# Full-attention layers: VectorE's queued pieces placed by an estimate of when TensorE finishes, and its own tiles' values planned a microsecond later

## The chip, the cores and the metric

One core of a Trainium2 chip runs the whole kernel: four layers of attention over 2048 tokens. The metric is the device time of one execution in microseconds (us). TensorE appears as PE (matmul) and PEld (weight load), VectorE as DVE, ScalarE as ACT, GpSimd as POOL, SyncE as SP.

## What is computed

The input x is 2048 x 512. Layers 0 and 2 attend in a sliding window of 256 tokens (A), layers 1 and 3 to all tokens (B). Each has 32 heads of 16 and adds its output to x:

```python
x = A_x
x = x + _A_ref(_layernorm(x, axis=-1), A_wqkv, A_wo)
x = x + _B_ref(_layernorm(x, axis=-1), B_wqkv, B_wo)
x = x + _A_ref(_layernorm(x, axis=-1), A_wqkv, A_wo)
x = x + _B_ref(_layernorm(x, axis=-1), B_wqkv, B_wo)
```

In `_B_ref`, per head:

```python
scores = jnp.einsum("bhqd,bhkd->bhqk", q, k) * scale
p = _softmax(scores, axis=-1)
o = jnp.einsum("bhqk,bhkd->bhqd", p, v)
```

## The kernel before

**Tiles of a full layer.** The work of a full layer is cut into 32 quads: 4 heads by one block of 512 queries, written (layer, block of queries, quad of heads) or as `1_3_4` in the names of tiles. Layer 1 goes block by block, layer 3 takes two quads of heads at a time through all four blocks. A quad goes through the 16 tiles of 128 keys (j). For each j there are two pairs of heads; each pair is one scores tile `s` of 128 x 1024 (8 matmuls, L760), which ACT turns into `e` by an exp (L768). Behind it follow the values of that j: 8 matmuls with the tile of V into the two accumulators `acc` (`values_of`, L839). The `s` tiles have two buffers in PSUM. When a quad's last values are in, `epilogue` reads the accumulators into `sa` on DVE (`join`, L438 and L439), transposes and scales.

**VectorE's own tiles.** One tile of keys, j = 7, can be taken off ACT: `unit` writes its scores to the single PSUM bank `halves` (called b in the profile, L778), DVE reads them (`d`, L784) and computes the exp by a polynomial, in two halves of six instructions (dm, d, dp, dp, dp, d, L792 to L804). Together with the reading an own tile is 13 DVE instructions, and a quad has at most two. `units` starts the next own tile if the planner still finds time before the quad's end. If two are in, their values are issued by `unit_values` as soon as the planner's clock has passed `u["at"]`, which is set from DVE's planned clock (L806: `vt_[0] + 0.4`), or, at the latest, right ahead of the quad's last values (`force`). If the second one isn't there three steps before the end, ACT makes it (`e <- s, lead`), and both values follow last.

**Side work.** Projections of this and the next layer, output projections (`wo`, `wo_part`) and the sums of squares for the bounds of the softmax run between the tiles. In a full layer each writes the same bank `halves`, which DVE must read (`j`, `vt`, `x`, `m`, `km`) before the next group may start. `Side` deals out one or two matmul groups of this work per step.

**What sets the order.** In the full layers PE's and DVE's instructions stand in the order in which the program's generators issue them. A planner keeps two clocks: `clock[0]`, PE's, is advanced by estimates (`spent`), and `vt_[0]`, DVE's, by `vec(us)`. DVE work that nothing waits for at once (halves of own tiles, scaling, norms, checks of the weights) is queued as pieces in five queues `VQ` by rank; `drain()` issues pieces while `vt_[0] <= clock[0] + AHEAD`, and a reading of a PSUM tile is issued directly, with a `vec` ahead of it:

```python
    def vec(us):

        vt_[0] = max(vt_[0], clock[0]) + us
...
        while vt_[0] <= clock[0] + AHEAD:
            order = VQ[:2] + VQ[3:4] if PH["mid"] else VQ if not UX or UX[0]["i"] <= PH["i"] else VQ[:3] + VQ[4:] + VQ[3:4]
            q = next((q for q in order if q and (q[0][2] is None or q[0][2]())), None)
            if q is None:
                return
            give(q)
```

All engines issue in order, so a reading whose operand PE has not finished holds up every piece behind it, and values whose operand DVE has not finished hold up every matmul behind them.

Of the kernel before, what the change touches and what calls it, by code (L numbers as in the profile page):

```python
# [39 lines left out]
WS = 16.0  # L40
W_MIN, W_MAX = 2.0 ** -7, 4.0
DJ = 7
AHEAD = 0.7
# [152 lines left out]
def fast_path(ctx, tc, flag, a_x, a_wqkv, a_wo, b_wqkv, b_wo, out):  # L196
# [34 lines left out]

        return "wait", clock[0] + us

    def vec(us):

        vt_[0] = max(vt_[0], clock[0]) + us

    def soon(chain, us, f, ok=None):

# [11 lines left out]
    def drain(upto=None):  # L251

        if upto is not None:
            if PH["mid"] and upto > 2:
                give(VQ[3])
            for q in VQ[:upto]:
                while q:
                    while q[0][2] and not q[0][2]():
                        PH["side"].one(True)
                    give(q)  # L260
            return
        while vt_[0] <= clock[0] + AHEAD:
            order = VQ[:2] + VQ[3:4] if PH["mid"] else VQ if not UX or UX[0]["i"] <= PH["i"] else VQ[:3] + VQ[4:] + VQ[3:4]
            q = next((q for q in order if q and (q[0][2] is None or q[0][2]())), None)
            if q is None:
                return
            give(q)

    def turns(chain, *ops):

# [161 lines left out]
                PH["busy"] = False  # L432
    TERMS = ((0, 0), (0, 1), (1, 0))

    def join(dst, ps, scale=1 / WS):

        vec(1.4)
        nc.vector.tensor_scalar(dst, ps[0], scale, None, op0=ALU.mult)  # L438
        nc.vector.scalar_tensor_tensor(dst, ps[1], scale, dst, op0=ALU.mult, op1=ALU.add)  # L439

# [119 lines left out]
    def squares(n, sqs):  # L560

        drain(1)
        vec(1.4)
        ph = bank()
        for t, sq in sqs.items():
            if PH["full"]:
                for r in range(2):
                    nc.tensor.matmul(ph[32 * t:32 * t + 32, r], hsum[R * r:R * r + R], sq[R * r:R * r + R],
                                     start=True, stop=True, skip_group_check=True)
            else:  # L570
                nc.tensor.matmul(ph[32 * t:32 * t + 32, :], hsum, sq, start=True, stop=True, skip_group_check=True)
        return ph
# [98 lines left out]
    def wo(l, c, tail):  # L671

        w = weights(l % 2, 3, f"o{l}_{c}")
        xs = load_x(l, c)
        yield wait(8)
        for i in range(4):
            ps = bank()
            yield from mms(ps, [(O[l, c, t][:, a, i * P:(i + 1) * P], w[:, t, b, :]) for t in range(NHT) for a, b in TERMS])
            k = 4 * c + i
            with tc.high_priority(HEAD_START):  # L680
                for p in ((ps[:, 0], ps[:, 1]) if PH["full"] else (ps,)):
                    nc.vector.scalar_tensor_tensor(xs[i], p, 1 / WS, xs[i], op0=ALU.mult, op1=ALU.add)
            nc.sync.dma_start(xd[k], xs[i])
            vec(1.4)
            soon(2, 0.9, lambda i=i: stats(l + 1, c, i, xs[i]))
            if i == 3 and not PH["full"]:
                yield from norm(l + 1, c, xs, tail)
            yield -MM if PH["full"] else -12 * MM
        OFREE.update((l, c, t) for t in range(NHT))
        if PH["full"]:  # L690
            yield from norm(l + 1, c, xs, tail)

    def wo_part(c, t):

        w = wp.tile([P, NC, 2, D], F16, name=f"wo_{c}_{t}", tag="w", bufs=WB)[:, 0]
        nc.sync.dma_start(w, wd[1, 3][:, t])
        xs = load_x(3, c)
        yield wait(4)
        o = O.pop((3, c, t))
        for i in range(4):  # L700
            ps = bank()
            yield from mms(ps, [(o[:, a, i * P:(i + 1) * P], w[:, b, :]) for a, b in TERMS])
            vec(1.4)
            k = 4 * c + i
            with tc.high_priority(HEAD_START):
                for p in ((ps[:, 0], ps[:, 1]) if PH["full"] else (ps,)):
                    nc.vector.scalar_tensor_tensor(xs[i], p, 1 / WS, xs[i], op0=ALU.mult, op1=ALU.add)  # L707
            nc.sync.dma_start(out[0, k * P:(k + 1) * P, :] if t == NHT - 1 else xd[k], xs[i])
            if i == 3:
                OFREE.add((3, c, t))  # L710
            yield -MM

    def epilogue(l, c, qd, a):

        n = f"{l}_{c}_{qd}"
        t, u = divmod(qd, 2)
        drain(2)
        ot = vp.tile([P, QC // 32, 32], F32, name=f"ot{n}", tag="oe", bufs=3)  # L720
        with tc.high_priority(HEAD_START if l % 2 else 0):
            if l % 2:
                a = vp.tile([P, QC], F32, name=f"sa{n}", tag="j")
                join(a, acc, 1.0)
                vec(0.7)
            nc.vector.transpose(ot.rearrange("p b r -> p (b r)"), a)  # L726

        def scaled():
            den = ot[:, :, DH]
            nc.vector.tensor_tensor(lmin, lmin, den, ALU.min)  # L730
            nc.vector.tensor_add(lsum, lsum, den)
            r = vp.tile([P, QC // 32], F32, name=f"r{n}", tag="r")
            nc.vector.tensor_scalar_max(r, den, L_MIN)
            nc.vector.reciprocal(r, r)
            if u == 0:
                OT[t] = vp.tile([P, QC // 32, 2, DH], F32, name=f"op{n}", tag="op", bufs=1)
            nc.vector.tensor_tensor(OT[t][:, :, u, :], ot[:, :, :DH], r[:, :, None].broadcast_to([P, QC // 32, DH]), ALU.mult)

        def parts():
            o = vp.tile([P, QC], F32, name=f"o{n}", tag="oe", bufs=3)  # L740
            nc.vector.transpose(o, OT.pop(t).rearrange("p b u d -> p (b u d)"))
            OL.append((l, c, t))
            hl = O[l, c, t] = wp.tile([P, 2, QC], F16, name=f"oh{n}", tag="ohl", bufs=OB)
            nc.vector.tensor_copy(hl[:, 0], o)
            nc.vector.tensor_tensor(hl[:, 1], o, hl[:, 0], ALU.subtract)
            ONR[l, c, t] = clock[0] + 4.5
        soon(1, 1.1, scaled)
        if u:
            soon(1, 1.6, parts, lambda: len(OL) < OB or OL[-OB] in OFREE)
# [21 lines left out]
    def unit(u):  # L771
# [8 lines left out]
        spent(0.27)  # L780
        PH["free"] = clock[0] + 1.5
        t = PH["ep"].tile([P, 2, QC], I32, name=f"d{n}", tag="d", bufs=2)
        vec(1.3)
        nc.vector.tensor_scalar(t, ps, SCALE * LOG2E * 2.0 ** 23, -2.0 ** 30, op0=ALU.mult, op1=ALU.max)  # L784
        u["e"].append(t.bitcast(F32))
        u["left"] += 2
# [55 lines left out]
    def unit_values(l, c, qd, force=False):  # L842
# [3 lines left out]
            return False  # L846
        if force:
            complete(u)
        elif len(u["e"]) < 2 or u["left"] or clock[0] < u["at"]:
            return False  # L850
        UX.popleft()
        values_of(l, qd, DJ, u["e"], False, False)
# [265 lines left out]
    def attention(l, works):  # L1118
# [5 lines left out]
        for t in range(NHT if l == 3 else 1):  # L1124
            for c in range(NQ):
                qds = range(2 * t, 2 * t + 2) if l == 3 else range(NQD)
                if l == 1:

                    sd = sd or Side((NT - 1) * NQD // 2, works[0], works[1], 0.33)
                    while ("Q", 1, c) not in DONE:  # L1130
                        sd.one(True)
                    settle()
                else:
# [44 lines left out]
                    ops = nxt  # L1178
                if l != 1 or c == NQ - 1:
                    sd.finish(l == 3 and (t, c) != (NHT - 1, NQ - 1))  # L1180
                if not win:
                    settle()
        flush(0)
        drain(5)
# [202 lines left out]
```

## Time and profile before

| What | us |
|---|---|
| Median of 3 runs | 2833.18 |
| Lowest and highest | 2832.88, 2838.49 |
| The profiled execution | 2838.99 |
| Its span, first to last instruction | 2837.2 |
| Mean granted TensorE clock over the span | 0.98 |

The span divides into layer 0 and setup (to about 495 us), layer 1 (to 1461), layer 2 (to 1808) and layer 3 with the end (to 2837). The groups of instructions by line give 2304 exps (L768), 22 exps with `lead`, and 106 own tiles (L784). "Idle before" a group is time in which its engine stood still, and the name behind an arrow is the instruction whose semaphore ended it. Only waits on an engine that others wait for in turn cost time.

### The profile page before, as it was taken

How to read it: one execution, taken by the hardware profiler on the slowest of the kernel's cores; microseconds unless marked ns; L12 is line 12 of the kernel's file. 1: busy time of each engine (PE TensorE's matmuls, PEld its weight loads, DVE VectorE, ACT ScalarE, POOL GpSimd, SP SyncE). 2: the span in 40 equal slices, each digit the busy share in tenths (PEclk: the TensorE clock that was granted, in tenths of full speed). 3: DMA queues.
4: the chain of work that ended last, by engine and by line, in shares of the span. 5: the costliest groups of instructions: out<-in, count | busy, mean ns of one | idle time of the engine just before them, and what ended most of it. 6: DMA issues, size and time to landing. Idle time of an engine off the chain costs nothing.

```text
span 2837.2 us, 112864 instructions
## 1 busy us (share of the span) xinstructions
PE 2528.1 (89%) x50177; PEld 1102.0 (39%) x50177; DVE 1991.0 (70%) x3817; ACT 2285.2 (81%) x2581; POOL 474.6 (17%) x1047
## 2 busy tenths in 40 slices
PE   7889999999998999999888899899899899888886
PEld 3333444444333444444333334434344344333332
DVE  5564454586778868878776566567778767777786
ACT  4565654999999998999865665699889889888886
POOL 1445551000000000000024776000000000000000
PEclk9999999999999999999999999999999999999999
DMA  8888856223223224223336654422332323333333
GB/s 274 237 234 238 242 178 203 60 78 108 87 88 96 66 96 109 92 83 103 103 116 207 170 151 140 141 83 87 94 92 88 94 85 101 95 100 105 123 104 122
DMA packets 335043, 359.71 MB, mean 127 GB/s; under 512 B 113617, under 2 KB 250321, under 8 KB 328145
## 3 DMA queue, kind: packets, MB, share of 16 engines
q1 hardware_dynamic: 334544, 352.40, 41.0%
q8 instruction: 394, 6.46, 0.9%
q14 instruction: 105, 0.85, 0.1%
HBM read 239.60 MB, written 96.99 MB: 119 GB/s over the span
## 4 chain that ended last, share of the span: by engine, by line
ACT 36%; PE 33%; DVE 16%; issue 9%; DMA 3%; POOL 2%; SPq 1%; ACTq 0%; DVEq 0%; POOLq 0%
ACT e L768 36%; PE b L425 9%; PE acc L839 9%; PE s L760 4%; PE b L422 3%; PE acc L941 3%; PE bs L425 2%; PE s L764 2%; DVE dp L803 1%; DVE dp L799 1%; DVE d L784 1%; DVE x L707 1%; DVE d L804 1%; DVE dp L800 1%; POOL e L931 1%
## 5 line engine op out<-in xcount | busy, mean ns | idle before, releaser
L768 ACT ACTIVATE e<-s 128x1024 f32<-128x1024 f32 (+2 forms) x2304 | 2138.4, 1044 | 257.8 <-PE s L760 139.5
L839 PE MATMUL acc<-e,vt 64*17 64x512 f32 x15536 | 1069.4, 593 | 0.2 <-issue 0.2
L760 PE MATMUL s<-qt,kt 64*32 64x512 f16 x15536 | 827.6, 382 | 114.7 <-ACT e L768 90.0
L760 PEld LDWEIGHTS <-kt 64*32 64x32 f16 x15536 | 376.8, 90 | 835.7 <-issue 759.4
L839 PEld LDWEIGHTS acc<-e,vt 64*17 64x17 f32 x15536 | 271.2, 93 | 86.7 <-issue 28.4
L934 POOL TENSOR_SCALAR_AFFINE_SELECT e<-e 128x256 f32<-128x256 f32 x512 | 220.8, 437 | 213.0 <-ACT e L768 211.8
L931 POOL TENSOR_SCALAR_AFFINE_SELECT e<-e 128x256 f32<-128x256 f32 x448 | 195.4, 443 | 116.7 <-ACT e L768 115.3
L941 PE MATMUL acc<-e,vt 128*17 128x384 f32 (+2 forms) x2816 | 205.8, 398 | 5.2 <-POOL e L931 4.0
L546 POOL TENSOR_TENSOR sq_h<-sp_h 128x512 bf16<-128x512 f16 x27 | 39.7, 1471 | 924.0 <-DVE sp_h L540 812.8
L546 POOL TENSOR_TENSOR sq<-sp 128x512 bf16<-128x512 f16 x28 | 40.9, 1461 | 868.0 <-DVE sp L540 795.4
L784 DVE TENSOR_SCALAR d<-b 128x1024 int32<-128x1024 f32 x106 | 129.3, 1220 | 79.0 <-PE b L778 78.8
L764 PE MATMUL s<-qt,kt 64*128 64x384 f16 (+2 forms) x1408 | 128.5, 280 | 56.0 <-ACT e L768 35.7
L425 PE MATMUL b<-xc,w 128*128 128x512 f16 x696 | 165.4, 389 | 6.2 <-DMA w<-wd 5.0
L803 DVE SCALAR_TENSOR_TENSOR dp<-dp,dm 128x512 f32<-128x512 f32 x212 | 152.3, 718 | 6.2
L799 DVE SCALAR_TENSOR_TENSOR dp<-dm 128x512 f32<-128x512 f32 x212 | 151.7, 715 | 0.2
L800 DVE SCALAR_TENSOR_TENSOR dp<-dp,dm 128x512 f32<-128x512 f32 x212 | 146.7, 692 | 7.4
L804 DVE SCALAR_TENSOR_TENSOR d<-dp,d 128x512 f32<-128x512 f32 x212 | 146.7, 692 | 7.2
L438 DVE TENSOR_SCALAR sa<-acc 128x512 f32<-128x512 f32 x64 | 44.2, 691 | 144.8 <-PE acc L839 144.3
L839 PE MATMUL acc<-d,vt 64*17 64x512 f32 x848 | 100.0, 606 | 38.3 <-DVE d L804 37.3
L425 PEld LDWEIGHTS <-w 128*128 128x128 f16 x816 | 77.4, 100 | 123.0 <-issue 37.5
L726 DVE STREAM_TRANSPOSE ot<-acc 128x512 f32<-128x512 f32 x64 | 45.6, 713 | 104.8 <-PE acc L941 104.8
L422 PE MATMUL b<-wo,oh 64*32 64x512 f16 x2592 | 111.3, 384 | 7.5 <-DVE x L707 4.6
(151 smaller groups left out, 2575.7 us busy)
## 6 DMA issues: line engine op xcount, KB each, us to landing
kt<-kf SPq DMA_DIRECT2D x128, 512.0 KB
qt<-qs SPq DMA_DIRECT2D x128, 256.0 KB
xd<-x SPq DMA_DIRECT2D x96, 256.0 KB
x<-xd SPq DMA_DIRECT2D x96, 256.0 KB
w<-wd SPq DMA_DIRECT2D x22, 1024.0 KB
kt<-kw SPq DMA_DIRECT2D x64, 256.0 KB
qs<-sp SPq DMA_DIRECT2D x48, 256.0 KB
wo<-wd SPq DMA_DIRECT2D x12, 1024.0 KB
```

The lines of the kernel that those rows point to most:

```text
L422: nc.tensor.matmul(ps[g:g + 32, r], a[k, g:g + 32], b[k], start=(i == 0), stop=(i == len(pairs) - 1), skip_group_check=True)
L425: nc.tensor.matmul(ps, a, b, start=(i == 0), stop=(i == len(pairs) - 1))
L760: nc.tensor.matmul(ps[g:g + 32, h], kt[R * h:R * h + R, pr, kc + g:kc + g + 32], qt[R * h:R * h + R, pr], start=True, stop=True, skip_grou ...
L764: nc.tensor.matmul(ps[:, h, s0:s0 + wd_], kt[R * h:R * h + R, pr, kc:kc + P], qt[R * h:R * h + R, pr, qc:qc + wd_], start=True, stop=True)
L768: nc.scalar.activation(e[:, :, w0:w1], ps[:, :, w0:w1], AF.Exp, scale=SCALE, **bias)
L799: nc.vector.scalar_tensor_tensor(p[0], f, POLY[3], f, op0=ALU.add, op1=ALU.mult)
L800: nc.vector.scalar_tensor_tensor(p[0], p[0], POLY[2], f, op0=ALU.add, op1=ALU.mult)
L803: nc.vector.scalar_tensor_tensor(p[0], p[0], POLY[1], m[0].bitcast(F32), op0=ALU.add, op1=ALU.mult)
L839: nc.tensor.matmul(acc[r][32 * h:32 * h + DH + 1, :], V[l, qd // 4, j // 8][k, j % 8, 4 * (qd % 4) + h, :], es[h // 2][k, h % 2, :], start ...
L931: nc.gpsimd.affine_select(v, v, pattern=[[0, 2], [-1, P]], compare_op=ALU.is_gt, fill=0.0, base=0, channel_multiplier=1)
L934: nc.gpsimd.affine_select(v, v, pattern=[[0, 2], [1, P]], compare_op=ALU.is_ge, fill=0.0, base=0, channel_multiplier=-1)
L941: nc.tensor.matmul(a[32 * h:32 * h + DH + 1, q * P:(q + nb) * P], V[l, (4 * c + j) // 4][:, j % 4, 4 * qd + h, :], es_[h // 2][:, h % 2, s ...
```

## The change

`vec` gets a second argument, the time after `clock[0]` at which the operand is estimated to be finished. In full layers it first issues queued pieces for as long as DVE's planned clock stays 0.4 us short of that time, and then books DVE as busy from that time on; in the windowed layers only the booking is done. The search for the next piece becomes a function, `give_next`, that `drain` uses too. The readings get these estimates: 1.3 us for joins, 2.0 for the join of `sa`, 1.0 for squares and x, 0.8 for own tiles; in `wo` the `vec` now also stands ahead of the reading, not behind it. The values of own tiles are held back until 1.0 us past `u["at"]`. Two calls of `settle` no longer happen while a side group is under way.

```diff
-    def vec(us):
-
-        vt_[0] = max(vt_[0], clock[0]) + us
+    def vec(us, after=0.0):
+
+        if PH["full"]:
+            while after and vt_[0] + 0.4 < clock[0] + after and give_next():
+                pass
+        vt_[0] = max(vt_[0], clock[0] + after) + us
...
-        while vt_[0] <= clock[0] + AHEAD:
-            order = VQ[:2] + VQ[3:4] if PH["mid"] else VQ if not UX or UX[0]["i"] <= PH["i"] else VQ[:3] + VQ[4:] + VQ[3:4]
-            q = next((q for q in order if q and (q[0][2] is None or q[0][2]())), None)
-            if q is None:
-                return
+        while vt_[0] <= clock[0] + AHEAD and give_next():
+            pass
+
+    def give_next():
+
+        order = VQ[:2] + VQ[3:4] if PH["mid"] else VQ if not UX or UX[0]["i"] <= PH["i"] else VQ[:3] + VQ[4:] + VQ[3:4]
+        q = next((q for q in order if q and (q[0][2] is None or q[0][2]())), None)
+        if q is not None:
             give(q)
+        return q is not None
...
-    def join(dst, ps, scale=1 / WS):
-
-        vec(1.4)
+    def join(dst, ps, scale=1 / WS, after=1.3):
+
+        vec(1.4, after)
...
         drain(1)
-        vec(1.4)
+        vec(1.4, 1.0)
         ph = bank()
...
+            vec(1.4, 1.0)
             with tc.high_priority(HEAD_START):
...
             nc.sync.dma_start(xd[k], xs[i])
-            vec(1.4)
...
-            vec(1.4)
             k = 4 * c + i
+            vec(1.4, 1.0)
...
-                join(a, acc, 1.0)
+                join(a, acc, 1.0, 2.0)
...
-        vec(1.3)
+        vec(1.3, 0.8)
...
-        elif len(u["e"]) < 2 or u["left"] or clock[0] < u["at"]:
+        elif len(u["e"]) < 2 or u["left"] or clock[0] < u["at"] + 1.0:
...
-                    while ("Q", 1, c) not in DONE:
+                    while ("Q", 1, c) not in DONE or pend and PH["busy"]:
...
-                if not win:
+                if not win and not PH["busy"]:
                     settle()
```

What it does to the order, at three places. The numbers at the ends of the names are those of the buffers; lines of the change stand 3 to 7 higher. First DVE at the end of quad (3,1,5), in layer 3: `d` are the own tiles 0 and 1 of the quad, `x` and `km` readings of the bank, `sa` the reading of the accumulators. Before:

```order
L707 SCALAR_TENSOR_TENSOR x3_2_46792<-b3_33668,x3_2_46792 128x512 x2
L792 TENSOR_SCALAR dm3_1_5_1_0_48105<-d3_1_5_1_47820 128x512
L793 TENSOR_SCALAR d3_1_5_1_47820<-d3_1_5_1_47820 128x512
L587 TENSOR_REDUCE km3_31320<-b3_33668 32x1
L799 SCALAR_TENSOR_TENSOR dp3_1_5_1_0_48141<-dm3_1_5_1_0_48105 128x512
L800 SCALAR_TENSOR_TENSOR dp3_1_5_1_0_48141<-dp3_1_5_1_0_48141,dm3_1_5_1_0_48105 128x512
L803 SCALAR_TENSOR_TENSOR dp3_1_5_1_0_48141<-dp3_1_5_1_0_48141,dm3_1_5_1_0_48105 128x512
L804 SCALAR_TENSOR_TENSOR d3_1_5_1_47820<-dp3_1_5_1_0_48141,d3_1_5_1_47820 128x512
L792 TENSOR_SCALAR dm3_1_5_1_1_48188<-d3_1_5_1_47820 128x512
```

After the last of these rows come five more of the second half of tile 1, and then `sa`. In the changed program:

```order
L806 SCALAR_TENSOR_TENSOR dp3_1_5_0_1_47801<-dm3_1_5_0_1_47790 128x512
L807 SCALAR_TENSOR_TENSOR dp3_1_5_0_1_47801<-dp3_1_5_0_1_47801,dm3_1_5_0_1_47790 128x512
L714 SCALAR_TENSOR_TENSOR x3_2_46612<-b3_33518,x3_2_46612 128x512 x2
L810 SCALAR_TENSOR_TENSOR dp3_1_5_0_1_47801<-dp3_1_5_0_1_47801,dm3_1_5_0_1_47790 128x512
L811 SCALAR_TENSOR_TENSOR d3_1_5_0_47597<-dp3_1_5_0_1_47801,d3_1_5_0_47597 128x512
L594 TENSOR_REDUCE km3_31170<-b3_33518 32x1
L714 SCALAR_TENSOR_TENSOR x3_3_46614<-b3_33518,x3_3_46614 128x512 x2
L445 TENSOR_SCALAR sa3_1_5_48045<-acc0_81 128x512
```

Tile 1 of this quad is no longer DVE's; ACT has an exp more (`e3_1_5_7_1<-s3_1_5_7_1,lead`), and `x3_3` is read ahead of `sa`, not behind it.

Second, PE at the end of layer 1, behind the last scores of quad (1,3,7): `b` is the bank, `w2_1_2` the weights of a projection for layer 2, `hsum` and `sq` the sums of squares that end it. Before, the 176 matmuls of the projection begin behind the scores:

```order
L760 MATMUL s1_3_7_15_1_28912<-qt1_3_7_27522,kt1_3_7_1_27526 32x512
L422 LDWEIGHTS w2_1_2_27609
L422 MATMUL b1_5731<-xc2_2_27668,w2_1_2_27609 32x512
L422 LDWEIGHTS w2_1_2_27609
L422 MATMUL b1_5731<-xc2_2_27668,w2_1_2_27609 32x512
```

In the changed program:

```order
L767 MATMUL s1_3_7_15_1_28993<-qt1_3_7_27621,kt1_3_7_1_27625 32x512
L575 LDWEIGHTS hsum_86
L575 MATMUL b1_5731<-sq2_1_2_0_27822,hsum_86 32x512
L575 LDWEIGHTS hsum_86
L575 MATMUL b1_5731<-sq2_1_2_0_27822,hsum_86 32x512
```

The projection's matmuls have moved into earlier quads of layer 1, and the squares follow the scores at once.

Third, DVE at the beginning of quad (3,0,2): `o` and `oh` are pieces that finish the heads' output of the quad before, `x3_6` a reading of the bank. Before:

```order
L737 TENSOR_TENSOR op3_3_0_38654<-ot3_3_1_39354,r3_3_1_39564 128x16x16
L707 SCALAR_TENSOR_TENSOR x3_6_37856<-b3_33668,x3_6_37856 128x512 x2
L741 STREAM_TRANSPOSE o3_3_1_39617<-op3_3_0_38654 128x512
L744 CAST oh3_3_1_39619<-o3_3_1_39617 128x512
L745 TENSOR_TENSOR oh3_3_1_39619<-o3_3_1_39617,oh3_3_1_39619 128x512
```

In the changed program:

```order
L744 TENSOR_TENSOR op3_3_0_38542<-ot3_3_1_39189,r3_3_1_39399 128x16x16
L748 STREAM_TRANSPOSE o3_3_1_39411<-op3_3_0_38542 128x512
L751 CAST oh3_3_1_39413<-o3_3_1_39411 128x512
L752 TENSOR_TENSOR oh3_3_1_39413<-o3_3_1_39411,oh3_3_1_39413 128x512
L714 SCALAR_TENSOR_TENSOR x3_6_37706<-b3_33518,x3_6_37706 128x512 x2
```

The piece of three instructions has gone ahead of the reading.

## The prediction

> **What bounds the kernel now.** I read the page's share lines first, then the chain, then stretches of the span by stage, and then who waits for whom inside the full layers, since the edited branches act only there.
>
> ```profile
> PE 2528.1 (89%) x50177; PEld 1102.0 (39%) x50177; DVE 1991.0 (70%) x3817; ACT 2285.2 (81%) x2581; POOL 474.6 (17%) x1047
> ACT 36%; PE 33%; DVE 16%; issue 9%; DMA 3%; POOL 2%; SPq 1%; ACTq 0%; DVEq 0%; POOLq 0%
> ```
>
> No engine holds the chain alone. The stages are more telling. In each row below stand the length of the stretch and then, per engine, its busy time and instruction count, the granted TensorE clock, and the DMA share. The rows are the 32 quads of layer 1, the end of layer 1, and the 32 quads of layer 3.
>
> ```profile
> 495.00:1447.00 952.00, 878.85 (x21969) 390.09 (x21976) 737.89 (x1361) 902.34 (x973) 38.73 (x29) 0.99 0.29 90
> 1447.00:1461.00 14.00, 8.87 (x251) 4.13 (x228) 9.36 (x16) 1.56 (x2) 3.58 (x5) 1.00 0.52 171
> 1808.00:2820.00 1012.00, 892.35 (x21622) 390.07 (x21613) 763.06 (x1298) 904.84 (x971) 39.72 (x27) 0.98 0.32 97
> ```
>
> ACT is busy 902 of 952 us in layer 1 and 905 of 1012 in layer 3, so ACT sets the pace, and its idle time (50 and 107 us) is what can be won. An exp tile costs ACT 902.34 / 973 = 0.93 us. Next, who makes ACT wait, first in layer 1 (495 to 1447 us), then in layer 3 (1808 to 2820 us); and for what PE waits in layer 3. The columns are total us, times, longest us.
>
> ```profile
> ACT e L768 <- PE s L760: 46.5, 37, 10.5
> ...
> ACT e L768 <- PE s L760: 93.0, 52, 6.9
> ...
> PE acc L839 <- DVE d L804: 25.9, 13, 3.2
> ```
>
> ACT waits for scores, and PE, which issues in order, brings them late when it stands before the values of a tile that VectorE still works on (d). One such place, quad (3,1,5), with the clock before, during and behind the wait, on PE, DVE, ACT:
>
> ```profile
> 2424.07 1.99 PE L839 MATMUL acc<-d,vt 64*17 64x512 f32 x12
> 2428.61 0.70 PE L839 MATMUL acc<-d,vt 64*17 64x512 f32 x2 [2.54 <-DVE d L804]
> ...
> 2427.86 0.69 DVE L804 SCALAR_TENSOR_TENSOR d<-dp,d 128x512 f32<-128x512 f32 x1
> 2431.90 0.69 DVE L438 TENSOR_SCALAR sa<-acc 128x512 f32<-128x512 f32 x1 [3.34 <-PE acc L839]
> ...
> 2432.39 3.83 ACT L768 ACTIVATE e<-s 128x1024 f32<-128x1024 f32 x4 [6.91 <-PE s L760]
> ...
> 2417.00:2424.00 7.00, 6.23 (x154) 2.59 (x142) 6.68 (x11) 7.00 (x9) 0.00 (x0) 1.00 0.37 115
> 2424.00:2428.60 4.60, 2.07 (x28) 0.23 (x8) 4.38 (x8) 1.49 (x2) 0.00 (x0) 1.00 0.62 205
> 2428.60:2433.00 4.40, 4.39 (x60) 1.96 (x61) 1.00 (x2) 0.60 (x1) 0.00 (x0) 0.61 0.01 4
> ```
>
> DVE finishes d at 2428.5, 4.5 us after PE began on its values. PE waits 2.54 us, then runs at a granted clock of 0.61 for 4.4 us, and ACT loses 6.91 us. A quad with one own tile ends otherwise: compare its last 12 us with the same stretch of (3,1,5).
>
> ```profile
> 2455.00:2467.00 12.00, 11.21 (x296) 4.98 (x295) 5.04 (x8) 11.72 (x13) 1.15 (x1) 1.00 0.43 123
> 2424.00:2436.00 12.00, 8.74 (x144) 3.11 (x132) 7.78 (x14) 5.09 (x6) 0.00 (x0) 0.86 0.32 102
> ```
>
> With one own tile ACT is idle only 12 - 11.72 = 0.28 us. So the waits sit at the ends of quads in which DVE has two own tiles.
>
> **The change, part by part.** The order of the changed program, counted per quad, says what the planner's numbers do. Own tiles fall from 106 to 93: quads with two of them from 20 to 11 in layer 1 and from 22 to 19 in layer 3.
>
> *ACT's added tiles.* 13 at 0.93 us: **+12.1 us**, 9.3 in layer 1 and 2.8 in layer 3. ACT bounds, so nothing hides them. DVE loses 13 x 13 instructions, off the bound.
>
> *Quads that lose an own tile.* Eleven in layer 1 and five in layer 3. These are ACT's waits at their ends, in order of time, where they pass 1.8 us (six of the eleven; the others hold under 1 us each and count nothing):
>
> ```profile
> 555.84 2.86 ACT L768 ACTIVATE e<-s 128x1024 f32<-128x1024 f32 x3 [1.82 <-PE s L760]
> 938.50 3.78 ACT L768 ACTIVATE e<-s 128x1024 f32<-128x1024 f32 x4 [2.37 <-PE s L760]
> 1086.15 4.69 ACT L768 ACTIVATE e<-s 128x1024 f32<-128x1024 f32 x5 [1.93 <-PE s L760]
> 1119.92 1.02 ACT L768 ACTIVATE e<-s 128x1024 f32<-128x1024 f32 x1 [4.93 <-PE s L760]
> 1240.06 5.61 ACT L768 ACTIVATE e<-s 128x1024 f32<-128x1024 f32 x6 [3.50 <-PE s L760]
> 1364.42 3.77 ACT L768 ACTIVATE e<-s 128x1024 f32<-128x1024 f32 x4 [10.53 <-PE s L760]
> 2053.16 3.77 ACT L768 ACTIVATE e<-s 128x1024 f32<-128x1024 f32 x4 [2.83 <-PE s L760]
> 2177.97 3.77 ACT L768 ACTIVATE e<-s 128x1024 f32<-128x1024 f32 x4 [3.59 <-PE s L760]
> 2495.54 1.02 ACT L768 ACTIVATE e<-s 128x1024 f32<-128x1024 f32 x1 [4.61 <-PE s L760]
> 2562.52 3.77 ACT L768 ACTIVATE e<-s 128x1024 f32<-128x1024 f32 x4 [5.78 <-PE s L760]
> ```
>
> Layer 1: 25.1 us. Layer 3, with the 6.91 above: 23.7 us. What a one-tile quad keeps, 0.28 x 11 = 3.1, goes off: **-45.7 us**. I take nearly all of it because DVE loses 13 instructions in each such quad: the two readings and eleven more that stood between the last scores and d.
>
> *Quads that gain an own tile.* Three: (1,2,5), (3,2,4), (3,3,4). A quad of layer 3 carries 93.0 / 32 = 2.9 us of ACT waits on the mean: **+8.7 us**. Bounds are 0.28 and 6.91 each.
>
> *The end of layer 1.* In the row 1447 to 1461 ACT does two tiles in 14 us while PE works off a leftover projection in two bursts with a DVE reading between them:
>
> ```profile
> 1447.04 2.35 PE L422 MATMUL b<-xc,w 64*32 64x512 f16 x80
> 1451.25 2.78 PE L422 MATMUL b<-xc,w 64*32 64x512 f16 x96 [1.86 <-DVE j L439]
> 1455.58 0.40 PE L568 MATMUL b<-sq,hsum 64*32 64x512 bf16 x6 [1.54 <-DVE j L439]
> 1457.71 0.39 PE L568 MATMUL b<-sq,hsum 64*32 64x512 bf16 x2 [1.74 <-POOL sq L546]
> 1457.72 1.24 PE L839 MATMUL acc<-e,vt 64*17 64x512 f32 x16
> ...
> 1460.61 0.50 PE L764 MATMUL s<-qt,kt 64*128 64x384 f16 x4
> ```
>
> In the changed order the sums of squares follow the last scores directly: these 176 matmuls now stand inside earlier quads. What stays is a few tenths for the squares, the wait for the last exp (about 1 us, one tile), and the values from 1457.72 to 1460.6, 2.9 us. That would take some 4.3 of the 14 us, so at most -9.7. DVE's last own tile had 10 us of cover here that is gone, so PE may wait about 2 us for it, as above. I take **-8 us**, bounds -9.7 and -5. The moved matmuls cost PE 2.35 + 2.78 = 5.1 us in the quads; ten more ACT tiles there give it 9.3 us, so I put them at nothing, and at +5.1 if that cover fails.
>
> *Readings and pieces in quads that keep their tiles.* The edit to `vec` cuts both ways. It hands out pieces while the reading is estimated not to be ready, but it also books VectorE as busy until then, so that the next drains hand out fewer. In the changed order of layer 3, 30 of the 64 x readings stand ahead of pieces that they stood behind, against one that moved the other way; three ends of quads got a piece ahead of `sa`. What DVE waits for over the whole span:
>
> ```profile
> DVE sa L438 <- PE acc L839: 144.3, 54, 8.7
> DVE d L784 <- PE b L778: 78.8, 70, 11.1
> DVE x L707 <- PE b L422: 22.0, 16, 2.7
> ```
>
> A piece before `sa` at the end of a quad fills part of a 2.7 us wait (144.3 / 54); an x read earlier may add a wait of up to a piece, but it also frees the one bank sooner. I take nothing for the sum. Below it: of ACT's 46.5 + 93.0 us, 48.8 are already counted, and half of the other 90.7 would be -45. Above it: see the slower rival. The values a microsecond later and the check on PH["busy"] touch only a few quads; their matmuls are the same, and I put them at nothing between -3 and +3 (the 1 us by three quads).
>
> **Sum**: 12.1 - 45.7 + 8.7 - 8 = -33 us. Against the profiled execution's 2838.99 (its span of 2837.2 and 1.8 around it) that is 2806; that execution lay 5.8 above the median of the runs shown, 2833.18, so the median to expect is **2800**.
>
> **The rivals.**
>
> 1. *The stalls move on* (17%). The quads with fewer own tiles are fine, but ones that keep two get later, since a changed plan shifts DVE's backlog instead of shrinking it. For it: DVE is busy 763 of 1012 us in layer 3 and each own tile still has to pass between readings. Against it: 13 x 13 instructions fewer. If half of the 45.7 comes back elsewhere, the sum is -10: 2823.
>
> 2. *Slower: readings placed earlier make d late* (18%). The x readings that now pass pieces make DVE wait, and 27 quads that keep two own tiles get d later by the piece passed, one to two instructions of the 0.69 us above, say 0.9 us. ACT's loss per us of PE wait is 6.91 / 2.54 = 2.7 at the worst; with 2, 27 x 0.9 x 2 = +49: 2849. It decides once most x readings wait: now 16 waits hold 22.0 us. It would undo the gain from about 33 / 49, two thirds of those quads. This is also the case in which the change doesn't do what its words say, as pieces would not go out ahead of readings.
>
> 3. *More* (15%). The filled waits before `sa`, j and vt bring d forward in the quads that keep two tiles, and half of the 90.7 us goes as well: -78, or 2755. I give it 2770 as its centre, since most such quads keep their order row for row.
>
> 4. PE as the bound instead of ACT would make the 13 tiles free and the 176 matmuls cost 5.1: -33 - 12.1 + 5.1 = -40, 2793, inside my own band. PE's 878.85 busy of 952 speaks for it; that ACT is busy 11.72 of 12 us at an undisturbed end of a quad speaks against it.
>
> 5. *A wait costs only itself* (10%). If PE came back from its waits at full speed, the five quads of layer 3 would yield PE's mean wait, 25.9 / 13 = 2.0 us each, 10 instead of 23.7 us, and the sum would be -19: 2814. Against it: the clock of 0.61 right behind a wait of 2.54 us, and 6.91 us lost by it. The Trainium skill, TensorE: Matmul & The Clock Gate, section "What's actually happening", states the rule on the other side: the clock halves only after an idle window of about 3.4 us, so that waits of 2 us would leave it whole. This trace differs from that, with 0.61 behind 2.54 us.
>
> **How the numbers follow.** The forecast, 2780 to 2818, has 50% (rivals 4 and 5 lie in it, the latter with 10 of the 50), "more" 15%, "moves on" 17% and slower 18%. A difference of 0.2%, 5.7 us, is about what a measurement of this kernel can tell from no change. Faster by that holds the forecast, "more", and half of "moves on": 0.73; the rest of that and the foot of the slower case are the same: 0.10; slower 0.17. The range leaves out a tenth on each side: it goes down into "more", to 2765, and up into the slower case, to 2843.
>
> **What would show it.** Right: ACT's waits on scores fall from 139.5 us in both full layers to about 95, the exp count rises by 13, ACT's busy time in each full layer rises by 9 and 3 us, and the 14 us stretch at the end of layer 1 shrinks to some 6. At the ends of quads (1,3,4), (3,1,5) and (3,3,5) ACT runs through at clock 1.00. Wrong: PE's waits on d in layer 3 stay at 25.9 us or rise, x readings wait far more than 22 us, or the new stretch behind layer 1's last scores holds a long wait for d. More ACT tiles than 13, or a PE wait for the bank that DVE reads later, would break the sum too.

## The result and the profile after

The changed kernel takes 2821.02 us (median of 5 runs, 2819.82 to 2824.31), the kernel before 2833.18 (5 runs, 2829.08 to 2838.49): a ratio of 0.9957, interval 0.9942 to 0.9972. It is 12 us faster; the forecast was 33, and 2800. The profiled execution of the changed kernel took 2821.02 us too, with a span of 2819.3 and a mean clock of 0.983. Lines of the changed kernel stand 7 higher than those of before. Its page, shares and chain:

```profile
PE 2520.6 (89%) x50177; PEld 1098.9 (39%) x50177; DVE 1885.5 (67%) x3648; ACT 2297.9 (82%) x2594; POOL 478.2 (17%) x1047
ACT 41%; PE 31%; DVE 12%; issue 9%; DMA 3%; POOL 2%; SPq 1%; ACTq 0%; DVEq 0%; POOLq 0%
```

ACT has its 13 exps more and 12.7 us more of busy time, DVE 106 us less. Next, by stretch, with the columns as in the prediction: layer 1 up to its last scores, the stretch behind them, and layer 3.

```profile
495.00:1449.40 954.40, 881.88 (x22152) 393.52 (x22160) 670.79 (x1257) 912.34 (x982) 41.96 (x31) 1.00 0.30 93
1449.40:1457.10 7.70, 4.49 (x64) 0.86 (x44) 4.72 (x9) 1.23 (x2) 0.45 (x2) 0.91 0.21 70
1797.00:2801.00 1004.00, 890.91 (x21598) 388.31 (x21597) 735.73 (x1259) 907.34 (x973) 40.02 (x27) 0.99 0.32 98
```

ACT's busy time rose by 10 us in layer 1 and by 2.5 in layer 3 (9 and 3 were forecast), and the stretch behind layer 1's last scores went from 14 to 7.7 us (some 6 were forecast). But layer 3 still leaves ACT idle for 1004.00 - 907.34 = 97 us, after 107. Who waits for whom over the whole span:

```profile
DVE sa L445 <- PE acc L846: 140.9, 51, 8.6
ACT e L775 <- PE s L767: 120.3, 77, 7.4
...
DVE x L714 <- PE b L429: 44.2, 36, 2.9
...
PE acc L846 <- DVE d L811: 40.7, 22, 3.4
```

ACT's waits fell from 139.5 to 120.3 us, not to 95. The readings of x wait twice as long as before (22.0 in 16 waits), and PE waits for d no less than before: 26.5 us in layer 3 after 25.9, and 40.7 over the span after 37.3. The prediction had named both as signs of being wrong.

**Where the time went.** The start of one `sa` reading to the start of the next is a quad's own time, and the quads can be sorted by what happened to their own tiles. The table sums these times over the profiled executions; the first quad of layer 1 has no such time, and that of layer 3 is in the last row. A second execution of the kernel before (e5) and the run that settled the matter (e14, below) stand beside it.

| Quads | before | e5 | after | after - before | forecast | e14 |
|---|---|---|---|---|---|---|
| 16 that lose an own tile | 506.0 | 505.8 | 476.6 | -29.4 | -45.7 + 14.9 = -30.8 | 473.6 |
| 3 that gain one | 92.2 | 91.7 | 92.5 | +0.3 | +8.7 - 2.8 = +5.9 | 90.5 |
| last quad of layer 1 | 39.1 | 39.2 | 33.3 | -5.8 | -8 | 30.9 |
| 24 that keep two | 739.1 | 736.1 | 757.2 | +18.1 | 0 | 731.6 |
| 17 that keep one | 502.2 | 502.0 | 507.6 | +5.4 | 0 | 501.2 |
| end of layer 1 to first `sa` of layer 3 | 378.8 | 375.7 | 371.1 | -7.7 | 0 | 369.5 |

With 1.1 us more in the last quad of layer 3 this gives -18.0, the difference of the two spans (2837.2 and 2819.3). That is more than the 12 us between the medians, because the profiled execution of the kernel before lay 5.8 us above its median. The forecast for the ACT tiles is put where it belongs, 0.93 us for each quad that lost or gained. The sum of the first three rows came nearly as forecast, -34.9 after -32.9. The two rows of quads that keep their tiles cost 23.5 us where the prediction took nothing.

### The profile page after: what moved, and what is told of

It is laid out like the page before. It is cut to its first block, busy times and chain, and to the rows that moved or that the text cites. A ratio compares the mean times of both kernels' runs of the same rounds, so it can differ in the third digit from the quotient of the medians.

```text
span 2819.3 us, 112722 instructions
## 1 busy us (share of the span) xinstructions
PE 2520.6 (89%) x50177; PEld 1098.9 (39%) x50177; DVE 1885.5 (67%) x3648; ACT 2297.9 (82%) x2594; POOL 478.2 (17%) x1047
## 4 chain that ended last, share of the span: by engine, by line
ACT 41%; PE 31%; DVE 12%; issue 9%; DMA 3%; POOL 2%; SPq 1%; ACTq 0%; DVEq 0%; POOLq 0%
ACT e L775 41%; PE b L432 10%; PE acc L846 7%; PE s L767 4%; PE acc L948 3%; PE b L429 3%; PE s L771 2%; PE bs L432 2%; DVE dp L810 1%; POOL e L938 1%; DVE d L811 1%; POOL e L941 1%; DVE dp L807 1%; DVE x L714 1%; DVE dp L806 1%
## 5 line engine op out<-in xcount | busy, mean ns | idle before, releaser
L775 ACT ACTIVATE e<-s 128x1024 f32<-128x1024 f32 (+2 forms) x2304 | 2139.2, 1045 | 233.6 <-PE s L767 120.3
L846 PE MATMUL acc<-e,vt 64*17 64x512 f32 x15640 | 1083.6, 591 | 1.3 <-DVE sa L445 1.3
L791 DVE TENSOR_SCALAR d<-b 128x1024 int32<-128x1024 f32 x93 | 113.4, 1220 | 92.5 <-PE b L785 92.5
L810 DVE SCALAR_TENSOR_TENSOR dp<-dp,dm 128x512 f32<-128x512 f32 x186 | 134.2, 722 | 5.0
L807 DVE SCALAR_TENSOR_TENSOR dp<-dp,dm 128x512 f32<-128x512 f32 x186 | 128.7, 692 | 6.5
L811 DVE SCALAR_TENSOR_TENSOR d<-dp,d 128x512 f32<-128x512 f32 x186 | 128.7, 692 | 6.4
L846 PE MATMUL acc<-d,vt 64*17 64x512 f32 x744 | 92.0, 598 | 41.6 <-DVE d L811 40.7
L806 DVE SCALAR_TENSOR_TENSOR dp<-dm 128x512 f32<-128x512 f32 x186 | 128.1, 688 | 0.2
L771 PEld LDWEIGHTS <-kt 64*128 64x128 f16 x1408 | 53.9, 95 | 160.9 <-issue 130.8
```

Of the source, the lines that this page charges most:

```text
L771: nc.tensor.matmul(ps[:, h, s0:s0 + wd_], kt[R * h:R * h + R, pr, kc:kc + P], qt[R * h:R * h + R, pr, qc:qc + wd_], start=True, stop=True)
L775: nc.scalar.activation(e[:, :, w0:w1], ps[:, :, w0:w1], AF.Exp, scale=SCALE, **bias)
L806: nc.vector.scalar_tensor_tensor(p[0], f, POLY[3], f, op0=ALU.add, op1=ALU.mult)
L807: nc.vector.scalar_tensor_tensor(p[0], p[0], POLY[2], f, op0=ALU.add, op1=ALU.mult)
L810: nc.vector.scalar_tensor_tensor(p[0], p[0], POLY[1], m[0].bitcast(F32), op0=ALU.add, op1=ALU.mult)
L811: nc.vector.scalar_tensor_tensor(x.bitcast(F32), p[0], POLY[0], x.bitcast(F32), op0=ALU.add, op1=ALU.mult)
```

## The experiments

Each time is a median, with its ratio to the kernel before on the same chip (2835.66 to 2837.43 us there) and the interval of the ratio.

**One own tile per quad, or none (e1, e2, e8).** e1 and e8 edit the kernel before, e2 the changed one:

```diff
-        if u["shut"] or len(u["e"]) == 2 or clock[0] < u["ready"]:
+        if u["shut"] or len(u["e"]) == 1 or clock[0] < u["ready"]:
```

In e8 the number is 0.

> The kernel before with at most one own tile per quad (64 instead of 106, the rest as it was; in this order the end of layer 1 also loses its leftover projection). Theory A, two own tiles in a quad make the values late and that is where ACT's waits come from: 42 tiles more on ACT cost 42 x 0.93 = +39 us, the 42 two-tile quads lose nearly all of their waits (123 us, less 0.3 each), the end of layer 1 gives 6 to 8: about -80, near 2754. Theory B, the waits only move to other readings of the bank: they stay, ACT's added tiles count in full, +39 less 8: near 2864.

> The changed kernel with at most one own tile per quad (64 instead of 93). Theory A: 25 two-tile quads lose 92 us of waits less 0.4 each and ACT gains 29 x 0.93 = 27 us of tiles: about -58 against the changed kernel, near 2763, and about the same as the kernel before with one tile. Theory B: +27, near 2848.

> The kernel before without own tiles at all: ACT makes all 2048 exps of the full layers. Against the kernel with one tile per quad (2768): 64 x 0.93 = +60 us of ACT, less at most the 48 us that ACT still waits for scores there. If one own tile per quad is worth its place, 2790 to 2828; if DVE's own tiles are a loss altogether, below 2768.

Measured: e1 2767.81 (0.9757, 0.9737 to 0.9777), e2 2763.27 (0.9743, 0.9723 to 0.9764), e8 2773.47 (0.9781, 0.9764 to 0.9797). So the second own tiles cost the kernel before 68 us, and all three beat the changed kernel. Theory A holds in e1 and e2; e1 lies 14 us above its number and e2 meets it. Even the first own tile is worth 6 us at most, with intervals that overlap, which missed e8's expectation of 2790 to 2828. In e1 PE's waits for d are almost gone, 8.1 us after 37.3:

```profile
ACT e L768 <- PE s L760: 47.8, 61, 4.9
...
PE acc L839 <- DVE d L804: 8.1, 3, 2.8
```

**The two halves of vec's edit, each alone (e3, e4).** e3 keeps the loop that hands out pieces and drops the booking; e4 the reverse.

```diff
-        vt_[0] = max(vt_[0], clock[0] + after) + us
+        vt_[0] = max(vt_[0], clock[0]) + us
```

```diff
-            while after and vt_[0] + 0.4 < clock[0] + after and give_next():
+            while False:
```

> The change with its loop that issues pieces, but DVE is booked as before from the planner's PE clock (105 own tiles, 42 two-tile quads, leftover projection of 192 matmuls at the end of layer 1). If the gain of the change comes from the smaller number of own tiles and the end of layer 1 (Theory A): same as before, 2828 to 2840. If it comes from pieces ahead of readings (Theory C): 2821 or lower, with DVE's waits on PE clearly below those of the kernel before.

> The change without its loop: DVE is booked from the estimated end of PE's work, but no piece is issued ahead of a reading (91 own tiles, no leftover at the end of layer 1). Theory A: about as the change, 2815 to 2826. Theory C: at or above the kernel before, 2833 or more, since only readings move ahead of pieces and nothing fills DVE's waits.

Measured: e3 2854.31 (1.0067, 1.0047 to 1.0087), e4 2835.89 (1.0005, 0.9991 to 1.0019). Both missed theory A's numbers on the slow side; for e4 theory C's held. But the planner chose 105 own tiles in e3 and 91 in e4, so neither is told apart from the number of tiles.

**The kernel before, once more (e5).** No edit.

> The kernel before once more, for a second trace. Every theory: 2829 to 2844. What it tells is how far layer 2 and the quads differ between two executions of one program: layer 2 lasted 7.7 us less in the trace of the change, and if it varies by as much here, that part is no effect of the change.

Measured: 2831.99, one run, span 2830.1. It is in the table above: the rows of quads repeat to within 3 us, and 3.1 of the 7.7 us by which the stretch between the full layers shrank are between two executions of one program. The other 4.6 were not forecast and stay unexplained; they don't need vec's argument, as e9 (below), which lacks it, has 368.8 us there.

**The kernel before with the changed kernel's own tiles (e6), and with the values later alone (e7).** CAP is a table of the changed kernel's count for each quad; it adds a line, so that lines behind it stand 1 higher:

```diff
-        if u["shut"] or len(u["e"]) == 2 or clock[0] < u["ready"]:
+        if u["shut"] or len(u["e"]) == CAP.get(u["quad"], 2) or clock[0] < u["ready"]:
```

```diff
-        elif len(u["e"]) < 2 or u["left"] or clock[0] < u["at"]:
+        elif len(u["e"]) < 2 or u["left"] or clock[0] < u["at"] + 1.0:
```

In e6 and e7 the two checks on PH["busy"] are missing, so that with this order sums of squares are written into the bank in the middle of a projection: that projection comes out with other values than the reference's, from the same number of instructions. Their times are therefore taken as hints, and e9 repeats e6 with the two checks.

> The kernel before, with a table that limits each quad to as many own tiles as the changed kernel has there (93 in all, quad by quad the same; no leftover at the end of layer 1), and the planner of before for everything else. Theory A, with the reordered readings as what ate the rest: the sum of the prediction without its rival, 33 us below the kernel before, 2795 to 2810, and the quads that keep two tiles as long as before. Theory D, that the quads with two tiles get longer because fewer own tiles push the waits into them, whatever stands ahead of what: as the changed kernel, 2816 to 2826.

> The kernel before with only the 1.0 us on the values (101 own tiles; 15 two-tile quads in layer 1 instead of 20; leftover of 40 matmuls instead of 176 at the end of layer 1; layer 3 unchanged in its tiles). Theory A: five quads give up their second tile at 2 us of waits less 0.93 each and the end of layer 1 gives some 5: 2824 to 2832. If the later values count by themselves, through PE's waits on d: below 2820.

Measured: e6 2786.67 (0.982, 0.9805 to 0.9836), below both ranges; e7 2818.58 (0.9946, 0.9928 to 0.9964), under theory A's range too and inside the other theory's (below 2820), though PE's waits on d fell only from 37.3 to 32.3 us. With the planner of before and the very same 93 own tiles the kernel is 34 us faster than the changed one (39 by the ratios). That is the missing sum, and it isn't the tiles. In e7 the planner went from 106 to 101 own tiles, so the microsecond acts through the tiles, too: against e5, the seven quads whose tiles it changes and the last quad of layer 1 give 9.7 of the 13.6 us between the spans (2830.1 and 2816.5).

**The same with the checks, and each half at the same tiles (e9, e10, e11).** e9 is e6 with the two checks of the change (no `settle` while a side group is under way). e10 is e3's edit with CAP (93 own tiles, quad by quad), e11 e4's with CAP (90).

> The kernel before, held to the changed kernel's own tiles quad by quad, and with the two checks on PH["busy"]: of the whole change only the argument of vec and the 1.0 us on the values are missing, and all values are computed as in the reference. Theory R (the reordering by vec's argument costs what is missing, some 34 us, and the checks cost nothing): 2782 to 2792, as e6 without the checks had 2786.67. Theory G (the checks, or the later values, carry the loss): 2805 or more.

> The changed kernel with the loop that hands out pieces ahead of a reading, without the booking of VectorE until the estimate, and with the changed kernel's 93 own tiles, quad by quad. Theory B (the loss is the booking's alone: the readings it moves ahead of pieces wait): 2780 to 2795, the time of the program without both. Theory P (pieces handed out ahead of a reading cost by themselves, the 20 us by which e3 lay above the kernel before at nearly its tiles): 2800 to 2815.

> The changed kernel with the booking and without the loop, held to at most the changed kernel's own tiles in each quad (90 by its own plan). Theory B (the booking puts readings ahead of pieces, VectorE waits in them, and the last d comes late): 2825 to 2840, with x readings waiting 35 us or more. Theory P (the loss is the loop's): 2780 to 2795.

Measured: e9 2776.34 (0.9796, 0.9779 to 0.9812), e10 2804.23 (0.9885, 0.987 to 0.9901), e11 2826.05 (0.9963, 0.9951 to 0.9975). Theory R holds: the checks cost nothing (e9 came out below its range, and 10 us below e6, with intervals that just overlap). Each half alone costs, against e9: the pieces 28 us, the booking 50 (both runs also have the 1.0 us on the values, which e9 lacks); so theories B and P are both right and both incomplete. They cost in different ways. With the pieces alone PE waits for DVE to have read the accumulators, a wait that e9 does not have at all:

```profile
DVE x L715 <- PE b L430: 28.9, 23, 3.0
...
PE acc L847 <- DVE sa L446: 17.7, 11, 1.8
...
PE acc L847 <- DVE d L812: 7.9, 7, 2.1
```

With the booking alone (e11) it waits for d, 46.5 us in 21 waits, after 12.3 in 10 in e9. The rows of e11, and that of e9:

```profile
PE acc L847 <- DVE d L812: 46.5, 21, 3.4
DVE x L715 <- PE b L430: 44.2, 33, 2.9
```

```profile
PE acc L840 <- DVE d L805: 12.3, 10, 2.5
```

**Which reading (e12, e13, e14).** Each takes the estimate from one kind of reading of the changed kernel, with CAP: e12 from x in layer 3 (L714; the other x readings keep it), e13 from the scores of own tiles (92 of them by its plan), e14 from `sa`.

```diff
-            vec(1.4, 1.0)
+            vec(1.4)
...
-        vec(1.3, 0.8)
+        vec(1.3)
...
-                join(a, acc, 1.0, 2.0)
+                join(a, acc, 1.0, 0.0)
```

> The changed kernel, with its 93 own tiles quad by quad, but without the estimate of 1.0 us at the readings of x in the full layers: no piece is handed out ahead of them and nothing is booked until it. Theory X (the x readings placed ahead of pieces carry the loss in layer 3): 2788 to 2803, with x waiting near the 21.6 us it had before and PE's waits on d under 20. Theory S (the 2.0 us at the join of sa carry it) or theory D (the 0.8 us at the own tiles' readings): 2814 to 2826.

> The changed kernel, held to at most its own tiles in each quad (92 by its own plan), without the estimate of 0.8 us at the reading of an own tile's scores. Theory D: 2788 to 2803, PE's waits on d under 20. Theories X and S: 2814 to 2826.

> The changed kernel, with its 93 own tiles quad by quad, without the estimate of 2.0 us at the join of sa: no piece is handed out ahead of sa and VectorE isn't booked until it. Theory S: 2788 to 2803, PE's waits on d under 20. Theories X and D: 2814 to 2826. If each of the three estimates carries a part, each of these runs lies between, near 2805 to 2813.

Measured: e12 2817.76 (0.9934, 0.9919 to 0.9948), e13 2831.02 (0.9982, 0.997 to 0.9994), e14 2779.21 (0.9804, 0.9788 to 0.982). It is `sa`: 42 us with one number, even below theory S's range, while x gives 3, with intervals that overlap, and the own tiles' reading, taken away, makes it 10 us slower (7 by the ratios), above its range. In e14 the waits are these:

```profile
DVE sa L446 <- PE acc L847: 154.5, 63, 8.6
...
ACT e L776 <- PE s L768: 81.5, 78, 5.9
...
DVE x L715 <- PE b L430: 21.5, 19, 2.9
...
PE acc L847 <- DVE d L812: 12.7, 11, 2.5
```

PE's waits on d fell from 40.7 us in the changed kernel to 12.7, and ACT's on scores from 120.3 to 81.5. The x readings still have their estimate in e14, and wait 21.5 us, about as before the change (22.0). In e12 those of layer 3 don't have it and wait 42.7 all the same:

```profile
DVE x L715 <- PE b L430: 42.7, 32, 2.9
```

So their longer wait was a consequence, not the cause.

**Is it enough alone, and does it need two tiles (e15, e16).** e15 has CAP (92 own tiles by its plan) and the estimate at `sa` alone; the defaults of the others are taken out. e16 is e2 with e14's edit.

> The changed kernel, held to at most its own tiles in each quad (92 by its own plan), with the estimate of 2.0 us at the join of sa alone; all other readings are planned as before. If sa's estimate alone is enough for the loss: 2812 to 2832, PE's waits on d at 35 us or more. If it needs the others beside it: 2776 to 2800.

> The changed kernel with at most one own tile in each quad, as e2, and without the estimate at the join of sa. If sa's estimate costs only where two own tiles follow it in the next quad: 2758 to 2767, the same as e2's 2763.27. If it costs 40 us at any number of tiles: 2720 to 2735.

Measured: e15 2844.89 (1.0025, 1.0012 to 1.0038), e16 2761.31 (0.9733, 0.9719 to 0.9747). The estimate at `sa` is enough by itself, and worse alone than with the others: it costs 69 us against e9 (65 by the ratios), above the range of its expectation, and the other estimates give 24 of them back (19 by the ratios). With one own tile per quad it costs nothing that these runs can tell: e16 and e2 are 2 us apart, with intervals that overlap. In e15 both ways of waiting are back:

```profile
PE acc L847 <- DVE d L812: 36.7, 17, 3.4
PE acc L847 <- DVE sa L446: 17.6, 11, 1.8
```

**How 2 us at `sa` make d late.** Quad (3,3,2) has two own tiles in both kernels. DVE in the changed kernel from `sa` of the quad before to its own `sa` (start, duration, engine, line, operation, and the idle time ahead):

```profile
2228.16 0.69 DVE L445 TENSOR_SCALAR sa<-acc 128x512 f32<-128x512 f32 x1 [3.22 <-PE acc L846]
...
2230.32 1.38 DVE L714 SCALAR_TENSOR_TENSOR x<-b,x 128x512 f32<-128x512 f32 x2
2232.23 1.22 DVE L791 TENSOR_SCALAR d<-b 128x1024 int32<-128x1024 f32 x1 [0.53 <-PE b L785]
2233.98 1.22 DVE L791 TENSOR_SCALAR d<-b 128x1024 int32<-128x1024 f32 x1 [0.53 <-PE b L785]
2235.12 0.18 DVE L737 TENSOR_TENSOR lmin<-lmin,ot 128x16 f32<-128x16 f32 x1
...
2237.46 1.42 DVE L714 SCALAR_TENSOR_TENSOR x<-b,x 128x512 f32<-128x512 f32 x2 [1.23 <-PE b L429]
2238.79 0.70 DVE L748 STREAM_TRANSPOSE o<-op 128x512 f32<-128x512 f32 x1
...
2250.27 0.69 DVE L445 TENSOR_SCALAR j_h<-b 128x512 f32<-128x512 f32 x1 [0.32 <-PE b L429]
...
2260.60 0.69 DVE L811 SCALAR_TENSOR_TENSOR d<-dp,d 128x512 f32<-128x512 f32 x1
2264.91 0.69 DVE L445 TENSOR_SCALAR sa<-acc 128x512 f32<-128x512 f32 x1 [3.62 <-PE acc L846]
```

And in e14:

```profile
2208.73 0.69 DVE L446 TENSOR_SCALAR sa<-acc 128x512 f32<-128x512 f32 x1 [3.22 <-PE acc L847]
...
2210.89 1.38 DVE L715 SCALAR_TENSOR_TENSOR x<-b,x 128x512 f32<-128x512 f32 x2
2212.18 0.17 DVE L738 TENSOR_TENSOR lmin<-lmin,ot 128x16 f32<-128x16 f32 x1
...
2213.20 1.22 DVE L792 TENSOR_SCALAR d<-b 128x1024 int32<-128x1024 f32 x1
2214.95 1.23 DVE L792 TENSOR_SCALAR d<-b 128x1024 int32<-128x1024 f32 x1 [0.53 <-PE b L786]
2216.09 0.70 DVE L749 STREAM_TRANSPOSE o<-op 128x512 f32<-128x512 f32 x1
...
2218.69 1.41 DVE L715 SCALAR_TENSOR_TENSOR x<-b,x 128x512 f32<-128x512 f32 x2
...
2238.82 0.69 DVE L812 SCALAR_TENSOR_TENSOR d<-dp,d 128x512 f32<-128x512 f32 x1
2241.49 0.69 DVE L446 TENSOR_SCALAR sa<-acc 128x512 f32<-128x512 f32 x1 [1.98 <-PE acc L847]
```

The work is the same. In e14 the scaling (lmin and what follows) goes out ahead of the first reading of d and fills that wait, and two pieces more (o and behind it dm and d of the first half) go ahead of the second x and fill that one. In the changed kernel, by the code, `sa` has booked DVE from 2.0 us past the planner's clock, so the next drains find DVE planned full and hand out nothing, and the readings come first; DVE then really stands still, 0.53 + 0.53 + 1.23 + 0.32 = 2.6 us against 0.5 (beside a wait of 1.38 us ahead of `km` in both). The last d of the quad ends 33.1 us after the first `sa` instead of 30.8. By the code, the clock that the 2.0 us are added to has already been moved past the quad's last values (the call that issues them and the epilogue begins with `spent(0.88)`), and here `sa` starts within 0.1 us of the end of PE's last matmuls on acc (2263.88 and 0.99). So the estimate seems to count what had been counted; that this is why 2.0 is too much was read from the code and this place, and not tried with other numbers than 0 and 2.0. Nor were the two halves of `vec` tried apart at `sa` alone; the waits speak for the booking, since the booking alone (e11) makes PE wait for d, as here, and the pieces alone (e10) make it wait for `sa`, which in the changed kernel comes to 1.3 us in all. PE, at the end of the quad in the changed kernel, first the wait and then the clock ahead of it and behind it:

```profile
2261.34 1.04 PE L846 MATMUL acc<-d,vt 64*17 64x512 f32 x2 [2.54 <-DVE d L811]
...
2263.88 0.99 PE L846 MATMUL acc<-e,vt 64*17 64x512 f32 x2
```

```profile
2257.00:2261.30 4.30, 1.81 (x36) 0.35 (x13) 4.13 (x7) 1.81 (x2) 0.00 (x0) 0.99 0.46 126
2261.30:2265.50 4.20, 4.16 (x64) 1.55 (x67) 0.59 (x1) 0.31 (x1) 0.00 (x0) 0.60 0.01 3
```

From `sa` to `sa` the quad takes 36.75 us, in e14 32.76: 2.3 us of delay on d became 4.0 us of the quad. In e14 d is ready when PE comes to it, and the clock stays whole:

```profile
2239.50:2244.00 4.50, 4.41 (x114) 2.23 (x108) 2.35 (x7) 3.33 (x5) 0.00 (x0) 1.00 0.41 117
```

## Why the forecast of 33 us became 12

The direction and the mechanism of the gain were right, and its terms add up nearly as forecast, in part by luck; one term, taken at nothing, cost 23.5 us.

- *Quads that lose an own tile, and the added ACT tiles*: -30.8 forecast, -29.4 measured. At (3,1,5) ACT now runs through, 11.99 of 12 us, at clock 1.00:

```profile
2405.00:2417.00 12.00, 11.23 (x277) 4.97 (x267) 7.23 (x11) 11.99 (x14) 0.00 (x0) 1.00 0.48 149
1353.00:1365.00 12.00, 9.62 (x222) 3.82 (x212) 10.62 (x18) 9.19 (x10) 1.54 (x1) 1.00 0.66 191
```

The second row is the end of (1,3,4), where ACT still loses 2.8 us; (3,3,5) runs through as well. That the sum fits is in part luck: layer 3 gave more than its share of the forecast (-22.1 in five quads, after 4.7 - 23.7 + 1.4 = -17.6 for the added exps, the waits and what a one-tile quad keeps), layer 1 less (-7.3 in eleven, after 10.2 - 25.1 + 1.7 = -13.2). One quad of layer 1, (1,2,7), even took 4.0 us more; it also does in e9 (3.3), so not through vec's argument.

- *Quads that gain one*: +5.9 forecast, +0.3 measured. The mean wait per quad was a poor price for three quads; all three were small.

- *End of layer 1*: -8 forecast, -5.8 measured. The uncovered wait for the last own tile came, and was longer than the 2 us I gave it:

```profile
1454.56 0.61 PE L846 MATMUL acc<-d,vt 64*17 64x512 f32 x2 [3.21 <-DVE d L811]
```

In e9, without the argument of vec, that quad takes 29.7 us (-9.4), near the bound of -9.7.

- **The step that failed**: "Readings and pieces in quads that keep their tiles", of which I wrote "I take nothing for the sum". It measured +23.5 us in the table. That is against the kernel before; against e9, which has the changed kernel's own tiles without vec's argument and without the 1.0 us on the values, the kernel loses 2821.02 - 2776.34 = 45 us. Taking the estimate at `sa` away (e14) gives 42 back, and 25.6 + 6.4 = 32 of these lie in the two rows of the table. The path that the prediction left out is this one: `sa` books DVE 2.0 us on, the pieces behind it go out later, the last d comes late, and PE waits for it (40.7 us, and 12.7 without the estimate). The bounds stood at -45 and +49, and the truth lay in the upper half. I chose the middle because two effects of unknown size pointed in opposite directions. The order held a hint: 30 x readings had gone ahead of pieces and one had gone behind, which says that fewer pieces were handed out, not more; what that costs it didn't say.

- *The values a microsecond later and the check on PH["busy"]*: nothing, give or take 3 us, was forecast. e7, with the microsecond alone, gains 15 us (0.9946 of before). It does so with five own tiles fewer, which the prediction counted in its other terms, so most of this (9.7 of 13.6 us against e5) is a matter of attribution; the rest isn't placed.

*The rivals.* The slower one, "readings placed earlier make d late", was the true mechanism, but with the wrong reading: not x (e12 moves 3 us) but `sa`, at the head of the quad. It didn't make the kernel slower because it was smaller than its 49 us: the quads that kept two tiles lost 18.1 us. "The stalls move on" gave the nearest number, 2823, by luck, for its reason is refuted: at the same tiles and with the old plan nothing moves on (in e9 the quads that keep two take 728.5 us, those that keep one 502.6). "More" (2770) is near what the change is without its number at `sa`: e14 has 2779.21. "PE as the bound" has against it the 11.99 of 12 us above, and that in e8, with no own tile, ACT waits for scores only 17.4 us in both full layers. "A wait costs only itself" falls too: it gave the five quads of layer 3 -10 + 4.7 = -5.3 us, and they measured -22.1; and behind a wait of 2.54 us PE again ran at 0.60. The Trainium skill, TensorE: Matmul & The Clock Gate, section "What's actually happening", puts the halving after an idle window of about 3.4 us; the measurement differs and decides.

Open is why the other estimates give back 24 us when `sa` has its own, and nothing when it has none (e14 lies 3 us above e9). A part shows in e13, 10 us slower without the own tiles' estimate (7 by the ratios): there PE waits for `sa` again, as in e15, after 1.3 us in the changed kernel.

```profile
PE acc L847 <- DVE sa L446: 12.3, 8, 1.7
```

Of the rest only the sums were measured, not the places.

## What to carry to other kernels

When a planner books an engine as busy until an estimated moment, look at what is behind that booking: here an estimate of 2.0 us at one reading per quad held back the pieces that would have filled the following waits, and the delay was paid again by whoever needed the last operand (2.3 us on d became 4.0 us of a quad). Where an edit has two effects of opposite sign and unknown size, count in the changed order which of them happened more often before you take the middle. And before changing when a stage runs, try it at half its amount: here one own tile per quad, the edit of one digit, was worth 68 us, more than five times what the change brought.

## What the runs showed of the hardware

At the two places shown, (3,1,5) before and (3,3,2) after, a wait of PE was paid twice: 2.54 us of idle time, and then more than 4 us of matmuls at a clock of 0.61 and 0.60. Over the whole span the slower clock weighs less. The same 50177 matmuls take PE 2528.1 us of busy time in the kernel before, at a mean clock of 0.980, and 2487.1 in e1, at 0.986; by the means alone, 2528.1 x 0.980 / 0.986 = 2512.7, the clock accounts for some 15 of these 41 us, an estimate. The rest is open, and e8 takes 2494.0 us at 0.989. And an own tile is worth far less than the exp it replaces. From e8 to e1, with 64 own tiles, ACT loses 45 us of busy time (2374.6 to 2329.7) and gets 30 us of waits for scores (17.4 to 47.8). The kernel gains 6 us by the medians, and 1.4 between the two profiled executions (spans of 2767.4 and 2766.0). The shares of e8, and of e1:

```profile
PE 2494.0 (90%) x50177; PEld 1097.9 (40%) x50177; DVE 1127.3 (41%) x2439; ACT 2374.6 (86%) x2687; POOL 479.4 (17%) x1047
```

```profile
PE 2487.1 (90%) x50177; PEld 1090.7 (39%) x50177; DVE 1645.1 (59%) x3271; ACT 2329.7 (84%) x2623; POOL 478.5 (17%) x1047
```

The waits of e8 on scores:

```profile
ACT e L768 <- PE s L760: 17.4, 20, 2.2
```
